# A decode product moved from VectorE to ScalarE and GpSimd, and half sums of k's exponentials for z in pairs three to nine

## The chip, the cores and the metric

The kernel runs on one core of a Trainium2 chip. The metric is the device time of one execution in microseconds (us); it is the median of several runs.

## The reference

Attention with a positive feature map feeds a two-layer network. In short, with 8 batches of 8 heads, 576 tokens, head size 64 and 128 features:

```python
def phi(x):
    proj = np.einsum('bhsd,df->bhsf', x, w_phi)
    proj = proj - np.max(np.abs(proj), axis=-1, keepdims=True)
    return np.concatenate([np.exp(proj), np.exp(-proj)], axis=-1)
q_p, k_p = phi(q), phi(k)
kv = np.einsum('bhsf,bhsd->bhfd', k_p, v)
z = np.sum(k_p, axis=2)
num = np.einsum('bhsf,bhfd->bhsd', q_p, kv)
den = np.einsum('bhsf,bhf->bhs', q_p, z)[..., None] + 1e-06
attn = num / den
...
x = attn.transpose(0, 2, 1, 3).reshape(4608, 512)
h = x @ w_in
g = np.maximum(h, 0.0) + alpha * np.minimum(h, 0.0)
out = g @ w_out
```

The weights `w_in` (512x2048) and `w_out` (2048x512) arrive as 64-bit numbers, two 32-bit words each, and are decoded on the chip.

## The kernel before

**Attention.** The work is cut into 32 pairs of heads, `attention_units(i)` for i = 0 to 31 (pair three of the title is i = 2). For a pair, `project(0)` and `project(1)` multiply ten tiles of tokens of k and q by `w_phi` on TensorE into PSUM (`pl` for the two short tiles, `pj` for eight). `pj` has one buffer. VectorE takes the largest magnitude (`m`, line 311) and subtracts it (`t`, line 312). ScalarE makes the exponentials of k (`xk`, four tiles, line 325, and `k`, the short one, line 320). `k_z` sums k's exponentials over the tokens by multiplying them with a matrix of ones on TensorE (line 365): for pairs i < 9 it takes all five tiles, four matmuls each. From pair 9 on, VectorE adds the five tiles up beforehand in `k_sum` (`y`, `z`, `z` again, lines 334, 338 and 341), and `k_z` has one tile left. `k_acc` makes kv (line 348), `kv_turn` and `q_turn` transpose (`kt`, `qt`), `q_exp` makes q's exponentials (`qf`, lines 402 and 404), `den` and `num` multiply them by z and kv (`d` line 431, `n` line 413). The denominators go through DRAM to be inverted (`r`, line 450) and spread (`rr`), and GpSimd multiplies them in (`s<-s,rr`, line 463).

**The two-layer network.** It runs in two passes over the tokens in chunks of 512. The first pass uses five of 16 slices of the hidden layer (`ffn1_units`) and is interleaved with the attention from pair 9 on. The second uses the other eleven and starts after the attention. Each operand is held as a high part and a low part (`gh` and `gl`, `xh` and `xl`), and three products are made of them.

**The decoding.** A block is 128x256 weights; there are 64, the first 20 within the attention-only start, two to a pair. `decode_load` brings in `raw`, whose last axis holds the low word and the high word. `decode_scale` (line 173) copies the high word with a factor on ScalarE. `decode_split` does four things on VectorE: a shift (181), an and-or that puts the sign in (182), a mask that leaves the exponent (183, `e`; the trace calls it `ew`), and a product of the low word with it (184). `decode_add` (189) adds that to the number on GpSimd. `decode_high` rounds it on ScalarE (123) and `decode_low` subtracts the rounded part on GpSimd (127). Blocks that do not stay in SBUF are written to `w_d`.

**The order.** Every step is put in a list with a due time by hand (`places(i)` for the attention; `WT` and `WL` for a block's steps after its time), and the list is sorted by it. The orders of TensorE, VectorE, ScalarE and SyncE are kept as they come; GpSimd's order is set by a scheduler.

Of the kernel before, what the change touches and what calls it, by code (L numbers as in the profile page):

```python
# [11 lines left out]
AF = mybir.ActivationFunctionType  # L12
ALU = mybir.AluOpType
# [39 lines left out]
XR_BUFS = 1  # L53
QH_BUFS = 2
ZP = 9


def places(i):
    early = i < ZP
    end = i >= NPAIR - 2  # L60
    return dict(
        ld=-1.90,
        lv=-0.80,
        p=(-0.9955 if early else -0.993, 0.0),
        ke=(-0.26, 0.0011),
        ks=(0.0015, 0.0022, 0.0026),
        kz=1.0002,
        ka=1.0012,
        ko=1.0025,
        kr=1.10,  # L70
        kc=1.16,
        q=(1.34, 1.50, 1.20),
        qe=(1.46, 1.62, 1.28),
        d=2.0004,
        ds=2.0008,
        n=2.005,
        s=2.0055,
        d9=2.25,
        dv=3.0016 if early else 3.20 if end else 2.80,
        rd=3.0017 if early else 3.21 if end else 2.82,  # L80
        rr=3.20 if early else 3.45 if end else 3.001,
        x=3.45 if early else 3.60 if end else 3.20,
        xs=3.90 if early else 3.85 if end else 3.45,
    )
# [24 lines left out]
def fused_kernel(ctx: ExitStack, tc: tile.TileContext, kq, v, w_phi, w_in, w_out, alpha, out):  # L109
    nc = tc.nc  # L110
    act, dve, pool, pe = nc.scalar, nc.vector, nc.gpsimd, nc.tensor
# [6 lines left out]
    def f(t):  # L118
        return t.bitcast(F32)
# [47 lines left out]
    wst = {}  # L167

    def decode_scale(ff, z, o, n):
        tag = f"w{ff}_{z}_{o}"  # L170
        raw = wraw.pop((ff, z, o))
        a = w1t.tile([P, n], U32, tag="wa", name=f"a{tag}", bufs=W_BUFS + 1)
        act.activation(f(a), raw[:, :, 1].bitcast(F32), AF.Copy, scale=2.0**-112)
        wst[ff, z, o] = [raw, a]

    def decode_split(ff, z, o, n):
        tag = f"w{ff}_{z}_{o}"
        raw, a = wst[ff, z, o][:2]
        lo, hi = raw[:, :, 0], raw[:, :, 1]
        e = w1t.tile([P, n], U32, tag="we", name=f"e{tag}", bufs=W_BUFS)  # L180
        dve.tensor_scalar(a, a, 3, None, op0=ALU.logical_shift_left)
        dve.scalar_tensor_tensor(a, hi, 0x80000000, a, op0=ALU.bitwise_and, op1=ALU.bitwise_or)
        dve.tensor_scalar(e, a, 0xFF800000, None, op0=ALU.bitwise_and)
        dve.scalar_tensor_tensor(f(e), lo, 2.0**-52, f(e), op0=ALU.mult, op1=ALU.mult)  # L184
        wst[ff, z, o] += [e]

    def decode_add(ff, z, o, n):
        _, a, e = wst[ff, z, o]
        pool.tensor_tensor(f(a), f(e), f(a), op=ALU.add)  # L189

    def decode_high(ff, z, o, n):
# [14 lines left out]
    def decode_store(ff, z, o, n):  # L206
# [4 lines left out]
    stages = dict(  # L211
        load=decode_load,
        scale=decode_scale,
        split=decode_split,
        add=decode_add,
        high=decode_high,
        low=decode_low,
# [54 lines left out]
    def attention_units(i):  # L272
        b, hp = divmod(i, NP)
        c = {}
# [51 lines left out]
            c["x", ch] = x  # L326

        def k_sum(step):
            if i < ZP:
                return  # L330
            x = c["x", 0].rearrange("p a h n f -> p (a h) (n f)")
            if step == 0:
                y = c["y"] = wk.tile([P, 4, 2 * FD], F32, tag="y", name=f"y{i}", bufs=1)
                dve.tensor_tensor(c["y"], x[:, :, : 2 * FD], x[:, :, 2 * FD :], op=ALU.add)
            elif step == 1:
                y = c["y"]
                c["zs"] = wk.tile([P, 4, FD], F32, tag="z", name=f"z{i}", bufs=1)
                dve.tensor_tensor(c["zs"], y[:, :, :FD], y[:, :, FD:], op=ALU.add)
            else:
                z = c["zs"]  # L340
                dve.tensor_tensor(z, z, c["x", 1].rearrange("p a h n f -> p (a h) (n f)"), op=ALU.add)
                c["z"] = z.rearrange("p (a h) f -> p a h f", a=2)
# [12 lines left out]

        def k_z():
            c["kv"] = ps_kv.tile([P, 3, FD], F32, tag="kv", name=f"kv{i}")
            if i < ZP:
                zs = [c["x", 0][:, :, :, j, :] for j in range(4)] + [c["x", 1][:, :, :, 0, :]]
            else:  # L360
                zs = [c["z"]]
            for j, z in enumerate(zs):
                for g in range(4):
                    h, a = divmod(g, 2)
                    pe.matmul(  # L365
                        c["kv"][32 * g : 32 * g + 32, 2],
                        lhsT=ones,
                        rhs=z[:, a, h, :],
                        start=j == 0,
                        stop=j == len(zs) - 1,  # L370
                    )
# [14 lines left out]
        def q_turn(h):  # L386
            pp, tag = (psf, "f") if i < ZP - 1 and h < 2 else (ps_m, "m")
            ps = c["qt", h] = pp.tile([P, 2 if h == 2 else 4, P], F32, tag=tag, name=f"qt{i}_{h}")
            if h == 2:
                for g in range(2):  # L390
                    pe.transpose(ps[:, g, :], c["t", 1][:, g, 0, :], ident)
            else:
                for j in range(4):
                    pe.transpose(ps[:, j, :], c["t", 1][:, h, 1 + j, :], ident)  # L394
# [70 lines left out]
        def store():  # L465
# [5 lines left out]
            (at["lv"], load_v),  # L471
            (at["ka"], k_acc),
            (at["kz"], k_z),
            (at["ko"], kv_out),
            (at["kr"], kv_turn),
# [14 lines left out]
        for n in range(3):  # L490
            us.append((at["ks"][n], lambda n=n: k_sum(n)))
            us.append((at["q"][n], lambda n=n: q_turn(n)))
            us.append((at["qe"][n], lambda n=n: q_exp(n)))
# [308 lines left out]
```

## Time and profile before

| | us |
|---|---|
| median of 3 runs | 1137.34 |
| lowest, highest | 1134.79, 1138.68 |
| the profiled execution | 1136.66 |
| its span in the trace | 1134.9 |

The page gives the busy time of each engine, its share in 40 slices, the transfers, the chain of work that ended last, and the costliest groups of instructions. The windows give the same busy times for chosen stretches, the timeline single instructions with the idle time before them and what ended it. Times count from the span's start. TensorE's clock stands at its full level (2.4 GHz, a granted clock of 1.00) after the first 50 us. The attention-only start lasts to about 105 us, the first pass to about 607 us, and the second pass to the end.

### The profile page before, as it was taken

What the parts mean: (1) busy time and instruction counts of PE and PEld (TensorE: products, weight loads), DVE (VectorE), ACT (ScalarE), POOL (GpSimd) and SP (SyncE); (2) the same over time, 40 slices, a digit from 0 to 9 for tenths busy, and PEclk for the clock granted to TensorE, in tenths of its full rate; (3) what the DMA queues carried; (4) which work ended last, traced back from release to release, by engine and by line L of the source; (5) the groups of instructions that cost most, each with busy time, mean ns of one, the idle gap of its engine ahead of it and who ended that gap; (6) DMA issues with size and microseconds to landing.
All of it is one profiled execution on the core that took longest, in us unless ns stands there. A gap on an engine that the chain in (4) does not pass through costs nothing.

```text
span 1134.9 us, 18362 instructions
## 1 busy us (share of the span) xinstructions
PE 1114.9 (98%) x7232; PEld 866.8 (76%) x7232; DVE 639.5 (56%) x978; ACT 561.2 (49%) x1149; POOL 214.5 (19%) x219
## 2 busy tenths in 40 slices
PE   7999999999999999999999999999999999999998
PEld 5766777777777777677778888888888888888886
DVE  7888867798788877835762432424242433333323
ACT  4777656666666765664553332424333333333332
POOL 1345332322424142243552000000000000000000
PEclk8999999999999999999999999999999999999999
DMA  5466264556446365466626130303030302020021
GB/s 188 142 184 216 80 194 147 171 163 205 145 163 199 94 214 168 146 197 213 231 74 211 69 112 1 111 1 111 1 112 1 111 1 80 33 79 33 3 72 38
DMA packets 74101, 133.68 MB, mean 118 GB/s; under 512 B 14624, under 2 KB 24480, under 8 KB 73376
## 3 DMA queue, kind: packets, MB, share of 16 engines
q1 hardware_dynamic: 71712, 122.48, 33.4%
q0 software_dynamic: 2016, 9.96, 2.6%
q8 instruction: 57, 0.93, 0.3%
q14 instruction: 28, 0.23, 0.1%
q10 hardware_dynamic: 288, 0.07, 0.0%
HBM read 93.92 MB, written 38.42 MB: 117 GB/s over the span
## 4 chain that ended last, share of the span: by engine, by line
PE 92%; DVE 4%; DMA 2%; ACT 1%; issue 0%; SPq 0%; ACTq 0%; DVEq 0%
PE h L503 11%; PE h L505 11%; PE h L504 11%; PE po L511 8%; PE po L509 8%; PE po L510 8%; PE kv L348 6%; PE pj L307 5%; PE n L413 5%; PE o L511 3%; PE o L509 3%; PE o L510 3%; PE d L431 3%; PE qt L394 2%; PE kv L365 2%; PE pl L307 1%
## 5 line engine op out<-in xcount | busy, mean ns | idle before, releaser
L240 DVE SCALAR_TENSOR_TENSOR g<-r,aln,g 128x512 f32<-128x512 f32 x144 | 111.0, 771 | 320.1 <-ACT g L236 319.8
L235 ACT ACTIVATE r<-h 128x512 f32<-128x512 f32 x144 | 86.5, 601 | 286.0 <-PE h L505 285.8
L127 DVE TENSOR_TENSOR gl<-g,gh 128x512 fp32r<-128x512 f32 x144 | 105.5, 732 | 73.0 <-ACT gh L123 72.5
L123 ACT CAST gh<-g 128x512 fp32r<-128x512 f32 x144 | 90.1, 625 | 88.1 <-DVE g L240 88.1
L236 ACT ACTIVATE g<-h 128x512 f32<-128x512 f32 x144 | 85.8, 596 | 2.8 <-DMA part_d<-os 2.8
L509 PE MATMUL po<-gh,wd 128*128 128x512 f32 x216 | 84.3, 390 | 0.0
L511 PE MATMUL po<-gl,wd 128*128 128x512 f32 x216 | 84.3, 390 | 0.0
L510 PE MATMUL po<-gh,wd 128*128 128x512 f32 x216 | 84.3, 390 | 0.0
L311 DVE TENSOR_REDUCE m<-pj 128x8 f32<-128x1024 f32 (+1 forms) x66 | 78.2, 1185 | 7.0 <-PE pj L307 6.7
L307 PE MATMUL pj<-w_sb,raw 64*128 64x128 f32 x1024 | 74.2, 286 | 7.8 <-DMA w_sb<-w_phi_dram 4.1
L307 PEld LDWEIGHTS pj<-w_sb,raw 64*128 64x128 f32 x1024 | 65.0, 194 | 21.4 <-issue 14.1
L189 POOL TENSOR_TENSOR aw<-ew,aw 128x256 f32<-128x256 f32 x64 | 56.7, 887 | 128.6 <-DVE ew L184 128.6
L312 DVE TENSOR_TENSOR t<-pj,m 128x1024 f32<-128x1024 f32 (+1 forms) x66 | 78.7, 1192 | 2.3
L509 PE MATMUL o<-gh,w 128*128 128x512 f32 x180 | 75.9, 422 | 1.9 <-ACT os L554 1.7
L503 PE MATMUL h<-xh,w 128*128 128x512 f32 x180 | 75.8, 421 | 0.0
L463 POOL TENSOR_TENSOR s<-s,rr 128x576 f32<-128x576 f32 x32 | 48.5, 1517 | 140.6 <-DMA rr<-rec_d 120.2
L511 PE MATMUL o<-gl,w 128*128 128x512 f32 x180 | 71.6, 398 | 3.2 <-DVE gl L127 3.0
L511 PE MATMUL po<-gl,w 128*128 128x512 f32 x180 | 70.3, 391 | 1.5 <-DVE gl L127 1.4
L404 ACT ACTIVATE qf<-qt 128x512 f32<-128x512 f32 x128 | 68.5, 616 | 6.3 <-PE qt L394 6.3
L505 PE MATMUL h<-xl,w 128*128 128x512 f32 x180 | 70.7, 393 | 0.0
L510 PE MATMUL o<-gh,w 128*128 128x512 f32 x180 | 70.6, 392 | 0.0
L504 PE MATMUL h<-xh,w 128*128 128x512 f32 x180 | 70.5, 392 | 0.0
(105 smaller groups left out, 2408.8 us busy)
## 6 DMA issues: line engine op xcount, KB each, us to landing
xr<-x_d SPq DMA_DIRECT2D x18, 1024.0 KB
raw<-kq_dram SPq DMA_DIRECT2D x31, 576.0 KB
v<-v_dram SPq DMA_DIRECT2D x32, 320.0 KB
w_d<-raww SPq DMA_DIRECT2D x38, 256.0 KB
rr<-rec_d SPq DMA_DIRECT2D x64, 144.0 KB
x_d<-s SPq DMA_DIRECT2D x32, 288.0 KB
part_d<-os SPq DMA_DIRECT2D x36, 256.0 KB
pt<-part_d SPq DMA_DIRECT2D x9, 1024.0 KB
```

The costliest lines, as they stand in the source:

```text
L123: return act.copy(dst, src)
L127: return eng.tensor_tensor(dst, src, f(hi), op=ALU.subtract)
L235: act.activation(st["r"], ps, AF.Relu, scale=-1.0)
L236: act.activation(st["g"], ps, AF.Relu)
L240: dve.scalar_tensor_tensor(g, st["r"], aln[:, ff : ff + 1], g, op0=ALU.mult, op1=ALU.add)
L307: pe.matmul(dst[h, j], lhsT=c["raw"][hs, ts], rhs=w_sb[hs], start=True, stop=True)
L503: pe.matmul(ps, lhsT=wt[0][:, ws], rhs=xh, start=n == 0, stop=False)
L504: pe.matmul(ps, lhsT=wt[1][:, ws], rhs=xh, start=False, stop=False)
L505: pe.matmul(ps, lhsT=wt[0][:, ws], rhs=xl, start=False, stop=n == NK - 1)
L509: pe.matmul(ps, lhsT=wt[2][:, ws], rhs=gh, start=first, stop=False)
L510: pe.matmul(ps, lhsT=wt[3][:, ws], rhs=gh, start=False, stop=False)
L511: pe.matmul(ps, lhsT=wt[2][:, ws], rhs=gl, start=False, stop=last)
```

## The change

In the decoding, ScalarE gets a second activation for a block: it converts the low word to a float and multiplies it by the constant factor, in place in `raw`. The product with `e` goes from VectorE to GpSimd, ahead of the addition there. For z, VectorE now makes `y` (two tiles of `xk` added to two others) for pairs 2 to 8 as well, and `k_z` takes `y` as two tiles and the short tile, three in all, where it took five.

```diff
+ZY = 2
...
         act.activation(f(a), raw[:, :, 1].bitcast(F32), AF.Copy, scale=2.0**-112)
+        act.activation(f(raw)[:, :, 0], raw[:, :, 0], AF.Copy, scale=2.0**-52)
         wst[ff, z, o] = [raw, a]
...
-        lo, hi = raw[:, :, 0], raw[:, :, 1]
+        hi = raw[:, :, 1]
...
         dve.tensor_scalar(e, a, 0xFF800000, None, op0=ALU.bitwise_and)
-        dve.scalar_tensor_tensor(f(e), lo, 2.0**-52, f(e), op0=ALU.mult, op1=ALU.mult)
         wst[ff, z, o] += [e]
 
     def decode_add(ff, z, o, n):
-        _, a, e = wst[ff, z, o]
+        raw, a, e = wst[ff, z, o]
+        pool.tensor_tensor(f(e), f(raw)[:, :, 0], f(e), op=ALU.mult)
         pool.tensor_tensor(f(a), f(e), f(a), op=ALU.add)
...
         def k_sum(step):
-            if i < ZP:
+            if i < ZY or i < ZP and step > 0:
                 return
...
-            if i < ZP:
+            if ZY <= i < ZP:
+                y = c["y"].rearrange("p (a h) (n f) -> p a h n f", a=2, n=2)
+                zs = [y[:, :, :, j, :] for j in range(2)] + [c["x", 1][:, :, :, 0, :]]
+            elif i < ZP:
                 zs = [c["x", 0][:, :, :, j, :] for j in range(4)] + [c["x", 1][:, :, :, 0, :]]
```

On VectorE, between the projections of pairs 5 and 6, before:

```order
L312 TENSOR_TENSOR t5_1_814<-pj5_1_817,m5_1_2_834 128x2x512
L450 RECIPROCAL r9_2_881<-d9_2_773 128x9
L181 TENSOR_SCALAR aw4_0_0_808<-aw4_0_0_808 128x256
L182 SCALAR_TENSOR_TENSOR aw4_0_0_808<-raww4_0_0_780,aw4_0_0_808 128x256
L183 TENSOR_SCALAR ew4_0_0_886<-aw4_0_0_808 128x256
L184 SCALAR_TENSOR_TENSOR ew4_0_0_886<-raww4_0_0_780,ew4_0_0_886 128x256
L311 TENSOR_REDUCE m6_0_0_901<-pj6_0_892 128x8
```

and with the change (all lines from the decoding on are one to five higher):

```order
L314 TENSOR_TENSOR t5_1_813<-pj5_1_816,m5_1_2_833 128x2x512
L336 TENSOR_TENSOR y5_872<-xk5_803 128x1024
L455 RECIPROCAL r9_2_874<-d9_2_770 128x9
L183 TENSOR_SCALAR aw4_0_0_806<-aw4_0_0_806 128x256
L184 SCALAR_TENSOR_TENSOR aw4_0_0_806<-raww4_0_0_778,aw4_0_0_806 128x256
L185 TENSOR_SCALAR ew4_0_0_879<-aw4_0_0_806 128x256
L313 TENSOR_REDUCE m6_0_0_893<-pj6_0_884 128x8
```

`y` stands ahead of the reciprocal of an earlier pair, and the product behind the mask is gone.

On ScalarE, between the transpose of pair 3's kv and its q exponentials, before:

```order
L384 COPY sf3_763<-kt3_756 128x384
L173 ACTIVATE aw3_0_256_775<-raww3_0_256_648 128x256
L402 ACTIVATE qf3_777<-qt3_2_768 128x2x64 x2
L123 CAST w3_93<-aw3_0_0_646 128x256
L404 ACTIVATE qf3_777<-qt3_0_782 128x512 x2
L404 ACTIVATE qf3_777<-qt3_1_791 128x512 x2
```

and with the change:

```order
L389 COPY sf3_760<-kt3_752 128x384
L174 ACTIVATE aw3_0_256_772<-raww3_0_256_651 128x256
L175 ACTIVATE raww3_0_256_651<-raww3_0_256_651 128x256
L407 ACTIVATE qf3_775<-qt3_2_765 128x2x64 x2
L124 CAST w3_93<-aw3_0_0_648 128x256
L409 ACTIVATE qf3_775<-qt3_0_780 128x512 x2
L409 ACTIVATE qf3_775<-qt3_1_789 128x512 x2
```

One activation more stands ahead of all six that make `qf`.

On GpSimd, the two blocks of one pair and the multiplication `s` of an earlier one, before:

```order
L189 TENSOR_TENSOR aw3_0_0_646<-ew3_0_0_724,aw3_0_0_646 128x256
L463 TENSOR_TENSOR s1_590<-s1_590,rr1_765 128x576
L127 TENSOR_TENSOR w3_93<-aw3_0_0_646,w3_93 128x256
L189 TENSOR_TENSOR aw3_0_256_775<-ew3_0_256_796,aw3_0_256_775 128x256
L127 TENSOR_TENSOR w3_93<-aw3_0_256_775,w3_93 128x256
```

and with the change:

```order
L190 TENSOR_TENSOR ew3_0_0_721<-raww3_0_0_620,ew3_0_0_721 128x256
L191 TENSOR_TENSOR aw3_0_0_648<-ew3_0_0_721,aw3_0_0_648 128x256
L468 TENSOR_TENSOR s1_590<-s1_590,rr1_762 128x576
L128 TENSOR_TENSOR w3_93<-aw3_0_0_648,w3_93 128x256
L190 TENSOR_TENSOR ew3_0_256_794<-raww3_0_256_651,ew3_0_256_794 128x256
L191 TENSOR_TENSOR aw3_0_256_772<-ew3_0_256_794,aw3_0_256_772 128x256
L128 TENSOR_TENSOR w3_93<-aw3_0_256_772,w3_93 128x256
```

Five instructions for a pair become seven; behind `s` a product stands between the subtraction of one block and the addition of the next.

## Rows read from the trace of the kernel before

**Rows 1.** The page, part 1: busy time, share of the span, instructions.
```profile
PE 1114.9 (98%) x7232; PEld 866.8 (76%) x7232; DVE 639.5 (56%) x978; ACT 561.2 (49%) x1149; POOL 214.5 (19%) x219
```

**Rows 2.** Windows: stretch, length, busy time of each engine, clock, DMA share, GB/s.
```profile
50.00:100.00 50.00, 48.62 (x617) 33.72 (x613) 42.01 (x74) 36.45 (x87) 21.54 (x24) 1.00 0.67 203
...
200.00:250.00 50.00, 50.00 (x419) 36.39 (x417) 40.49 (x59) 32.80 (x71) 17.10 (x15) 1.00 0.54 171
```

**Rows 3.** The chain in order of time: start, duration, what (z's matmuls).
```profile
35.27 1.23 PE kv L365 x40
...
66.99 1.23 PE kv L365 x40
...
77.57 1.23 PE kv L365 x40
...
101.29 1.23 PE kv L365 x40
```

**Rows 4.** Timeline, TensorE, one pair: start, duration, line, tiles, idle time before.
```profile
66.92 1.08 PE L365 MATMUL kv<-xk,ones 128*32 128x128 f32 x32
...
67.82 0.40 PE L365 MATMUL kv<-k,ones 128*32 128x128 f32 x8
...
69.12 1.95 PE L348 MATMUL kv<-xk,v 128*64 128x256 f32 x16
```

**Rows 5.** Timeline, ScalarE, the same pair.
```profile
65.00 0.44 ACT L173 ACTIVATE aw<-raww 128x256 f32<-128x256 f32 x1
...
65.34 0.43 ACT L402 ACTIVATE qf<-qt 128x128 f32<-128x128 f32 x2
...
65.95 2.07 ACT L404 ACTIVATE qf<-qt 128x512 f32<-128x512 f32 x4
```

**Rows 6.** Timeline at 89 us, where `d` waited for `qf`.
```profile
89.43 1.56 ACT L404 ACTIVATE qf<-qt 128x512 f32<-128x512 f32 x3
...
91.04 0.14 PEld L431 LDWEIGHTS d<-qf,sf 128*32 128x32 f32 x4 [0.33 <-ACT qf L404]
...
91.65 1.95 PE L348 MATMUL kv<-xk,v 128*64 128x256 f32 x16
```

**Rows 7.** Timeline, VectorE and GpSimd, the same pair as in rows 4.
```profile
65.54 0.29 DVE L181 TENSOR_SCALAR aw<-aw 128x256 uint32<-128x256 uint32 x1 [0.99 <-ACT aw L173]
...
66.73 0.43 DVE L184 SCALAR_TENSOR_TENSOR ew<-raww,ew 128x256 f32<-128x256 uint32 x1
...
70.51 0.21 DVE L450 RECIPROCAL r<-d 128x9 f32<-128x9 f32 x1
70.62 0.83 POOL L127 TENSOR_TENSOR w<-aw,w 128x256 fp32r<-128x256 f32 x1 [0.79 <-ACT w L123]
...
70.90 0.83 DVE L182 SCALAR_TENSOR_TENSOR aw<-raww,aw 128x256 uint32<-128x256 uint32 x1
```

**Rows 8.** `y` at 105 us; then lines 334 and 189: ns min/median/max, first and last start.
```profile
104.95 1.68 DVE L334 TENSOR_TENSOR y<-xk 128x1024 f32<-128x1024 f32 x1
105.52 2.25 POOL L127 TENSOR_TENSOR xl<-xr,xh 128x512 fp32r<-128x512 f32 x1
...
L334 DVE TENSOR_TENSOR y<-xk x23: 1215/1216/2212, 105.0 to 480.1; 128x1024 f32<-128x1024 f32 x23
...
L189 POOL TENSOR_TENSOR aw<-ew,aw x64: 717/738/1648, 20.1 to 597.3; 128x256 f32<-128x256 f32 x64
```

**Rows 9.** Timeline: a reciprocal on VectorE, and the `s` that uses it.
```profile
59.94 0.21 DVE L450 RECIPROCAL r<-d 128x9 f32<-128x9 f32 x1
...
66.76 1.68 POOL L463 TENSOR_TENSOR s<-s,rr 128x576 f32<-128x576 f32 x1 [3.94 <-DMA rr<-rec_d]
```

**Rows 10.** Timeline, later: two waits of TensorE and the product ahead of one.
```profile
152.10 0.50 PE L509 MATMUL o<-gh,w 128*128 128x512 f32 x1 [1.72 <-ACT os L554]
...
540.27 0.42 DVE L184 SCALAR_TENSOR_TENSOR ew<-raww,ew 128x256 f32<-128x256 uint32 x1
...
541.36 0.50 PE L511 MATMUL po<-gl,w 128*128 128x512 f32 x1 [1.38 <-DVE gl L127]
```

## The prediction

> **What bounds the kernel now.** I read the page's busy times first: TensorE is busy for 1114.9 of 1134.9 us, VectorE, ScalarE and GpSimd for 56%, 49% and 19% [rows 1]. Idle time of the other three therefore costs nothing, unless TensorE waits for it. Second, the windows: between 50 and 100 us TensorE is busy for 48.62 of 50 us and VectorE for 42.01, in the steady stretch at 200 us for 50.00 and 40.49 [rows 2]. So the attention-only part at the start is the place where VectorE, too, is nearly full. Third, the chain of waits in that part: it consists of TensorE alone, and a pair takes 77.57 - 66.99 = 10.58 us [rows 3], from one group of `z` matmuls to the next. I call this the period of a pair. Whatever lengthens or shortens it between about 35 and 105 us lengthens or shortens the whole, because TensorE is full behind it.
>
> All durations below come from the profiled execution (1136.66 us, its span 1134.9). The median of the three runs is 1137.34, 0.68 us above it; the forecast is made for the median. About 0.3% (3.4 us) is what a measurement of this kernel can tell from no change.
>
> **Part 1: z by half sums on TensorE.** For pairs 2 to 8 the 16 matmuls of `xk` with `ones` become 8. Each shows as two records. The 32 records start at 66.92 and the next group at 67.82 [rows 4]: 0.90 us. Half of that is 0.45 us a pair, 3.15 us for seven pairs. TensorE is on the path, so this is the whole possible gain of this part. It is 0.28% of the time.
>
> **Part 2: the product's first half on ScalarE.** 64 more activations of 128x256, two a pair. The trace has no strided write of this kind; the nearest row is the activation of the same form, which starts at 65.00 with the next instruction following at 65.34 [rows 5]: 0.34 us of ScalarE's time each. Lower bound 0 (if it fits into a wait), upper 0.45 (its duration). I take 0.34, the row of the same shape and stride. Where it stands matters more. One of the two stands between the scaling and the six activations that make `qf`, the last of which ends at 65.95 + 2.07 = 68.02 [rows 5]. The `d` matmuls read `qf`. How tight that is can be read at 89 us, where `d` really waited: the last `qf` ended at 89.43 + 1.56 = 90.99, and the first matmul after `d` started at 91.65 [rows 6], 0.66 us later. In the undisturbed pair the same matmul starts at 69.12 [rows 4], 1.10 us behind its `qf`; so the slack is 0.44 us. Part 1 takes 0.45 us of it away (TensorE arrives earlier) and part 2 another 0.34. TensorE then waits 0.45 + 0.34 - 0.44 = 0.35 us a pair, and of the 0.45 us saved 0.10 remain: period 10.48. This is the step on which I rest most: the saving is given back at `d`.
>
> **Part 3: VectorE.** In a period of 10.58 VectorE waits 0.99 us, before the shift of the second block [rows 7], and is busy for 9.59. The change takes away two products of 0.43 each [rows 7] and adds one `y`, 1.22 us where nothing disturbs it [rows 8]. That gives 9.59 - 0.86 + 1.22 = 9.95 us. It would fit into 10.48 with 0.53 to spare. `y` itself is used a whole period later, so TensorE doesn't wait for it; what it delays is the projection's reduce and subtract behind it, and TensorE's next projection waits for those, since `pj` has one buffer.
>
> **Part 4: GpSimd, and what it does to VectorE.** 64 more products of 128x256 on GpSimd. The row for the same shape with contiguous operands is 0.74 us [rows 8]; with one operand of stride two the trace shows none. Bounds 0.72 (the shortest of that row) and 1.65 (the longest); I take 0.74. By itself this costs nothing: in the stretch from 50 to 100 us GpSimd is busy for 21.54 of 50 [rows 2], and ten products would add 7.4. But a VectorE instruction and a GpSimd one that both work in SBUF do not overlap. The shift-and-or at 70.90 took 0.83 us instead of 0.43, beside a GpSimd subtraction that had begun at 70.62 [rows 7]; and the `y` at 104.95 took 1.68, while the GpSimd subtraction that began at 105.52 took 2.25 us [rows 8]. The Trainium skill says in "SBUF — State Buffer", section "SBUF: two separate sides", that the two engines share a pair of ports by an exclusive lock, held for the whole instruction, and that the loser is fully blocked; these two pairs of rows agree.
>
> So I ask whether `y` meets GpSimd. `s<-s,rr` starts when its `rr` lands, 6.82 us after the reciprocal (59.94, then 66.76), and lasts 1.68 [rows 9]. The reciprocal now stands behind `y`, so `s` moves about 1.2 us later in the pair. Behind it stand a subtraction, the new product and the addition: 66.8 + 1.2 + 1.7 (`s`) + 0.7 (the subtraction) puts the product at about 70.4 and the addition at 71.1 in the terms of the pair shown, and `y` begins where the reciprocal stands now, at 70.51 [rows 7]. A collision with the product or the addition is to be expected in each pair. One more collision costs VectorE up to 0.74: 9.95 + 0.74 = 10.69 us. Two would give 11.43. None gives 9.95, and then the period is the 10.48 of part 2. I take one, since the additions that follow the second block's split lie under reads of PSUM, which the rows don't show to collide. Period 10.69 instead of 10.58: 0.11 us lost a pair.
>
> **Part 5: the later blocks.** 44 of the 64 blocks are decoded after the start, under a TensorE that is full. There only TensorE's few waits count: for `gl` of VectorE at 541.36 (1.38 us), with a product of 0.42 us just before that `gl`, and for ScalarE at 152.10 (1.72 us), which waits for a transfer and doesn't change [rows 10]. Without the product `gl` comes about 0.4 us earlier. Lower bound: four such waits for `gl` shrink by 0.43 each, -1.7 us. Upper bound: they grow by a GpSimd instruction each, +3.0. I take -0.4, for the one place where the removed product stands next to the wait.
>
> **The sum.** Pairs 2 to 6 (their `z` matmuls stand from 35.27 to 77.57 us [rows 3]): 5 x 0.11 = +0.55. Pair 7: its `d` is the one that waited for the late `qf` [rows 6], so an earlier TensorE only waits longer: 0. Pair 8: its `z` lies at 101.29 us [rows 3], next to the full stretch; I let it keep its 0.45. The later blocks: -0.4. Together -0.3 us, 1136.4 in terms of the profiled execution, **1137.0 us** in terms of the median: no change that can be told.
>
> **Rivals.**
> *The saving goes through.* If the new activation hides in a wait of ScalarE, and GpSimd's instructions fall under VectorE's reads of PSUM, nothing stands against part 1. For it: VectorE's own sum, 9.95, is below 10.13 (10.58 - 0.45), so with no collision it can follow. Against it: the slack of 0.44 at `d`. Time: 3.15 us less, and two later waits shorter by 0.43: 1137.34 - 4.0 = 1133.3. Chance 0.18.
>
> *VectorE becomes the bound through collisions.* `y` waits for a GpSimd instruction, another enters between `y` and the shift behind it, and so the sum reaches 9.95 + 2 x 0.74 = 11.43 us a pair, 0.85 more than now. It decides from the point where collisions cost more than 0.63 us a pair (9.95 + 0.63 = 10.58). For it: three GpSimd instructions (product, addition, subtraction) stand in a row at that place. Against it: a longer period lets GpSimd finish before the next `y`. Five pairs of it make +4.25, and one later wait longer by 0.74: 1137.34 + 5.0 = 1142.3. Chance 0.20. The lock named above, if it holds for every one of these instructions, is the rule under which this rival wins.
>
> That the change doesn't do what it says is excluded by the order of the instructions: TensorE's groups of 16 are groups of 8 in seven pairs, and VectorE has one instruction less in each block.
>
> **How the numbers follow.** My forecast has a chance of 0.62, the two rivals 0.18 and 0.20. The range reaches from a little below the first (1133.3, with one later wait less) to the second: 1132.8 to 1142.5. The forecast's own range, between periods of 10.48 and 11.0, is 1135.5 to 1140.0, all of it within 0.3%. So faster by more than 0.3% has 0.18, within 0.3% 0.62, slower 0.20.
>
> **What would show it.** Part 1 is right if the `kv<-y,ones` groups take about 0.45 us. Part 2 is right if `d` waits for `qf` in the steady pairs, by about 0.35 us where VectorE is not the later one; wrong if the chain still shows no wait there. Part 4 is right if `y` lasts well over 1.22 us in pairs 3 to 8 and TensorE's `pj` waits for `t`; wrong if `y` has its bare duration. If the period between 35 and 78 us comes out at 10.13, the first rival holds; at 11 or more, the second. The prediction as a whole is wrong if the stretch up to 105 us changes by more than 3 us, or if the waits behind 450 us do.

## The result, and the profile after

The changed kernel took 1139.56 us (median of 10 runs, 1138.45 to 1141.98) against 1137.31 for the kernel before beside it (10 runs): a ratio of 1.0023 with an interval of 1.0014 to 1.0033. It is slower by 2.25 us. That is small, but outside the interval, where the forecast was no change, a little on the fast side. The profiled execution has a span of 1137.7 us, 2.8 more than before.

The page, part 1, of the changed kernel [answers to rows 1]:

```profile
PE 1114.8 (98%) x7120; PEld 865.7 (76%) x7120; DVE 621.2 (55%) x921; ACT 582.3 (51%) x1213; POOL 272.8 (24%) x283
```

Work moved as the change says: VectorE has 18 us less, ScalarE 21 more, GpSimd 58 more. TensorE has 112 instructions less and the same busy time. (The busy time is modelled, and a matmul that waits inside a group counts as busy.) So the question is where it stood still.

The windows of the changed kernel [answers to rows 2]:

```profile
50.00:100.00 50.00, 46.86 (x541) 31.79 (x537) 45.20 (x70) 40.22 (x100) 31.76 (x34) 1.00 0.67 202
200.00:250.00 50.00, 49.91 (x412) 36.63 (x410) 38.31 (x56) 33.69 (x75) 19.66 (x19) 1.00 0.55 175
```

In the attention-only part TensorE is busy for 1.8 us less than before in the same window, 46.86 against 48.62. The steady stretch has hardly moved.

To find the places, I compared the start of the first group of `kv<-xk,v` in each pair, after minus before (from the two timelines; a step in this offset is time lost or gained between two pairs):

| pair | 1 | 2 | 5 | 6 | 7 | 8 | 9 | 11 | 14 | 29 | 30 | end |
|---|---|---|---|---|---|---|---|---|---|---|---|---|
| offset, us | -0.87 | -0.98 | -1.29 | -0.39 | -0.06 | -0.06 | +1.79 | +2.09 | +2.42 | +2.41 | +1.78 | +2.8 |

The changed kernel is 1.29 us ahead at pair 5, 0.87 of it from ahead of pair 1, and loses 3.1 between pairs 5 and 9. Behind that the account is nearly even: +0.6 up to pair 14, -0.6 at pair 30, +1.0 up to the end.

**The gain.** The chain of the changed kernel, steady pairs [answers to rows 3]; start, duration, what:

```profile
34.39 0.79 PE kv L370 x24
35.19 1.30 PE d L436 x16
36.49 2.31 PE kv L350 x20
...
44.87 0.79 PE kv L370 x24
45.66 1.30 PE d L436 x16
```

The same step of the chain before:

```profile
36.50 0.97 PE d L431 x16
```

`z` takes 0.79 us instead of 1.23, so 0.44 is saved. `d` takes 1.30 instead of 0.97, so 0.33 is given back: it waits for `qf` between its matmuls (the run with the new activation behind `qf`, below, shows this). The period is 44.87 - 34.39 = 10.48 instead of 10.58.

**The loss.** The timeline of the changed kernel between pairs 8 and 9; start, duration, engine, line, and in brackets the idle time before and what ended it:

```profile
102.50 1.43 POOL L468 TENSOR_TENSOR s<-s,rr 128x576 f32<-128x576 f32 x1 [2.82 <-DMA rr<-rec_d]
103.88 1.28 POOL L128 TENSOR_TENSOR xl<-xr,xh 128x512 fp32r<-128x512 f32 x1
104.86 1.38 DVE L336 TENSOR_TENSOR y<-xk 128x1024 f32<-128x1024 f32 x1
105.13 1.71 POOL L128 TENSOR_TENSOR w<-aw,w 128x256 fp32r<-128x256 f32 x1
106.80 1.18 POOL L190 TENSOR_TENSOR ew<-raww,ew 128x256 f32<-128x256 f32 x1
108.06 0.72 POOL L191 TENSOR_TENSOR aw<-ew,aw 128x256 f32<-128x256 f32 x1
108.82 0.40 ACT L124 CAST w<-aw 128x256 fp32r<-128x256 f32 x1 [3.18 <-POOL aw L191]
109.13 0.40 ACT L446 ACTIVATE ds<-d 128x288 f32<-128x288 f32 x1
109.43 0.71 ACT L322 ACTIVATE k<-t 64x256 f32<-64x256 f32 x2
110.04 0.46 ACT L380 COPY ks<-kv 128x384 f32<-128x384 f32 x1
110.56 0.55 PE L385 MATMUL kt<-ident,ks 128*128 128x128 f32 x3 [1.79 <-ACT ks L380]
```

The same block before:

```profile
104.83 0.72 POOL L189 TENSOR_TENSOR aw<-ew,aw 128x256 f32<-128x256 f32 x1
105.58 0.40 ACT L123 CAST w<-aw 128x256 fp32r<-128x256 f32 x1 [0.45 <-POOL aw L189]
106.81 0.46 ACT L375 COPY ks<-kv 128x384 f32<-128x384 f32 x1
```

Read it from the bottom. TensorE's `kt` waits 1.79 us for `ks`. `ks` depends on nothing new, but ScalarE's order is fixed, and three places ahead of it stands the rounding `cast w`, which waited 3.18 us for GpSimd's addition. The addition comes 3.2 us later than before (108.06 against 104.83). About 1.0 of it is `s`, which started at 102.50 instead of 101.51, since its `rr` landed later (the reciprocal now stands behind `y`; that was not tried apart). Another 1.0 is the subtraction `w` of the other block, which used to take 0.72, began 0.27 us after `y` and took 1.71. Behind it came the new product, which took 1.18; the addition began 1.26 after it. GpSimd's order is otherwise that of the kernel before: the second `xl` stands behind the addition in both. At 74.33 us the same chain costs 0.94.

In the last stretch the rounding stands ahead of other work of ScalarE:

```profile
525.47 0.40 ACT L124 CAST raww<-aw 128x256 fp32r<-128x256 f32 x1 [4.47 <-POOL aw L191]
525.78 1.07 ACT L559 COPY os<-o 128x512 f32<-128x512 f32 x2
526.41 0.50 PE L514 MATMUL o<-gh,w 128*128 128x512 f32 x1 [0.79 <-ACT os L559]
...
556.68 0.41 ACT L124 CAST raww<-aw 128x256 fp32r<-128x256 f32 x1 [7.11 <-POOL aw L191]
...
558.12 0.50 PE L508 MATMUL h<-xh,w 128*128 128x512 f32 x1 [1.07 <-ACT g L238]
```

And the two waits of [rows 10], in the changed kernel, with what ScalarE waited for ahead of the first, at 153 us:

```profile
153.07 0.62 ACT L124 CAST xh<-xr 128x512 fp32r<-128x512 f32 x1 [3.00 <-DMA xr<-x_d]
154.23 0.50 PE L514 MATMUL o<-gh,w 128*128 128x512 f32 x1 [2.05 <-ACT os L559]
...
543.07 0.50 PE L516 MATMUL po<-gl,w 128*128 128x512 f32 x1 [0.92 <-DVE gl L128]
```

**The theory (A).** What stands ahead of TensorE's producer (the instruction whose result it waits for) in ScalarE's order decides. GpSimd's addition is late, the rounding waits for it, and `ks` (later `os` and `g`) waits behind the rounding, without needing it. The same holds for ScalarE's cast of x, which waits for a transfer with `qf` and `os` behind it. **The rival:** the load and the collisions of VectorE and GpSimd decide, so the order on ScalarE has no price. The expectations call the rival theory B, or name one that fits the run.

### The profile page after: what moved, and what is told of

Its sections match the earlier page's. It is cut to its first block, busy times and chain, and to the rows that moved or that the text cites. A ratio compares the mean times of both kernels' runs of the same rounds, so it can differ in the third digit from the quotient of the medians.

```text
span 1137.7 us, 18267 instructions
## 1 busy us (share of the span) xinstructions
PE 1114.8 (98%) x7120; PEld 865.7 (76%) x7120; DVE 621.2 (55%) x921; ACT 582.3 (51%) x1213; POOL 272.8 (24%) x283
## 3 DMA queue, kind: packets, MB, share of 16 engines
q0 software_dynamic: 2016, 9.96, 2.5%
## 4 chain that ended last, share of the span: by engine, by line
PE 83%; DMA 6%; DVE 5%; ACT 3%; issue 2%; POOL 1%; SPq 0%; DVEq 0%; ACTq 0%; POOLq 0%
PE h L508 11%; PE h L510 11%; PE h L509 10%; PE po L516 8%; PE po L514 8%; PE po L515 8%; PE kv L350 5%; PE pj L309 5%; PE n L418 4%; PE o L516 3%; PE o L514 3%; PE o L515 3%; PE d L436 2%; PE qt L399 2%; DMA rr<-rec_d 2%
## 5 line engine op out<-in xcount | busy, mean ns | idle before, releaser
L190 POOL TENSOR_TENSOR ew<-raww,ew 128x256 f32<-128x256 f32 x64 | 56.8, 887 | 103.8 <-DVE ew L185 40.5
```

## The experiments

### One part of the change at a time

The part on z alone: the decoding is that of the kernel before. Against the changed kernel, the main lines:

```diff
-        act.activation(f(raw)[:, :, 0], raw[:, :, 0], AF.Copy, scale=2.0**-52)
...
+        dve.scalar_tensor_tensor(f(e), lo, 2.0**-52, f(e), op0=ALU.mult, op1=ALU.mult)
...
-        pool.tensor_tensor(f(e), f(raw)[:, :, 0], f(e), op=ALU.mult)
```

> Only the z part (y for pairs 2 to 8 on VectorE, two tiles fewer on TensorE); the decoding is as before. Theory A (the loss comes from ScalarE's queue: a rounding that waits for GpSimd's late addition stands ahead of ks, and TensorE's kt waits for ks): no added wait of kt near 110 us; VectorE is busy 9.59 + 1.22 = 10.81 us a pair and so sets a period of about 10.8 in pairs 2 to 6, the rest as before; 1137.3 to 1138.8 us. Theory B (the additional y on VectorE makes the loss): the whole loss is here, 1139.5 us or more, and TensorE's waits after 105 us grow as in the changed kernel.

Measured: 1141.39 us, ratio 1.0038 (1.0024 to 1.0052), slower than before. The time is the one that theory B named (1139.5 or more); theory A had named 1137.3 to 1138.8. Two waits of TensorE from its timeline:

```profile
56.43 1.16 PE L308 MATMUL pj<-w_sb,raw 64*128 64x128 f32 x16 [0.47 <-DVE t L313]
...
92.77 0.68 PE L435 MATMUL d<-qf,sf 128*32 128x288 f32 x4 [1.66 <-ACT qf L408]
```

A part of the loss is VectorE's, as B has it. With both products and `y`, VectorE is too long: `pj` waits for `t`, 0.19, 0.47, 0.46 and 0.72 us, and the offset to the kernel before goes from +0.35 at pair 2 to +1.18 at pair 6, where z should have gained. The larger step, +2.57 from pair 6 to pair 7, is at the second row: `qf` stands there behind a cast of x that waited 3.20 us for its transfer, and behind the gap the granted clock reads 0.92 and 0.74 in the windows from 90 to 100 us. (Why that transfer was late was not tried apart.) No wait of `kt` for `ks` over 0.1 us is left, as A expected. So `y` alone doesn't make the waits at `kt`, but it has a price of its own while both products stay on VectorE.

The decoding alone: `y` only from pair 9 on, as before.

```diff
-ZY = 2
+ZY = 9
```

> Only the decoding part (low words scaled on ScalarE, product on GpSimd); z as before. Theory A: the wait of kt for ks near 109 us is there (1 us or more), the second half of the first pass gains about 1 us of waits for ScalarE, the period up to 80 us stays at 10.57 (ScalarE's 0.34 fits into the slack of 0.44); 1139 to 1140 us. Theory B: no loss, 1137.3 us or less, since VectorE only loses work.

Measured: 1143.15 us (4 runs), ratio 1.005 (1.0032 to 1.0067). Both theories had named less (A 1139 to 1140). The period stayed at 10.57, and the time went where TensorE waited for ScalarE: 1.24 us for `ks` at 99.6 (not near 109, where it was expected; there it lost nothing), 0.95 for `qf` at 90.9, 1.97 for `os` at 530, and at 154 us

```profile
154.58 0.56 PE L514 MATMUL o<-gh,w 128*128 128x512 f32 x1 [2.51 <-ACT os L559]
```

with this window right behind:

```profile
155.00:160.00 5.00, 5.00 (x28) 3.85 (x27) 0.43 (x3) 3.92 (x7) 3.88 (x4) 0.67 0.71 220
```

After that idle time the granted clock was 0.67 of full speed for 5 us, 1.65 us of work; behind the wait at 530 it read 0.66, another 1.7. The two falls make about half of the 6.8 us by which this trace is longer than the one before. Each part alone is slower than the kernel before: z needs the time that the decoding frees on VectorE, and the decoding by itself adds waits and saves TensorE nothing.

### The order on ScalarE

The rounding behind `ks`: for the second block of each pair up to 10 it comes later in the program.

```diff
+WE = dict(WT, high=0.504)
...
-        return [(t + (WT if t < TL else WL)[k], ...
+        return [(t + (WE if t < 11 and t % 1 > 0.25 else WT if t < TL else WL)[k], ...
```

> The changed kernel, with the rounding of each odd block of the first 20 put behind ks in ScalarE's queue. Theory A: the waits of kt for ks (0.94, 0.54 and 1.79 us at 73, 97 and 109 us) fall below 0.3 each, and the time falls by about 2 us to 1137.5 us. Theory B: the waits stay or come back as waits for VectorE, 1139.5 us.

Measured: 1139.96 us, ratio 1.0023 (1.0011 to 1.0035): no gain in the time, where A had named 1137.5 and the rival 1139.5. In the trace, all waits of `kt` for `ks` are gone, and pair 9 starts at -1.31 instead of +1.79 us. The rounding still waits for the addition, but `ks` stands ahead of it now:

```profile
105.27 0.47 ACT L381 COPY ks<-kv 128x384 f32<-128x384 f32 x1
107.03 0.41 ACT L125 CAST w<-aw 128x256 fp32r<-128x256 f32 x1 [1.28 <-POOL aw L192]
...
151.49 0.62 ACT L125 CAST xh<-xr 128x512 fp32r<-128x512 f32 x1 [3.74 <-DMA xr<-x_d]
...
152.64 0.58 PE L515 MATMUL o<-gh,w 128*128 128x512 f32 x1 [2.80 <-ACT os L560]
```

The last two rows say where most of it went. (Of the 3.4 us from pair 9 to pair 11, 0.8 go ahead of pair 10.) At 151 us ScalarE's cast of x waits for its transfer, which doesn't come earlier because TensorE does (151.49 against 150.94 before), and `os` stands behind that cast. TensorE's gap grew from 1.72 to 2.80, and behind it the clock was low:

```profile
150.00:155.00 5.00, 2.36 (x6) 1.90 (x7) 0.21 (x1) 3.52 (x7) 2.16 (x2) 0.79 0.74 180
155.00:160.00 5.00, 5.00 (x53) 3.43 (x54) 2.20 (x5) 1.98 (x4) 3.02 (x3) 0.87 0.64 198
```

From pair 11 on the offset is +2.09, as in the changed kernel. Theory A is right on the cause at 109 us, but a second wait of the same kind, and the fall of the clock behind it, took all of it back.

ScalarE's new activation of the second block behind `qf`:

```diff
+WE = dict(WT, lows=0.13)
...
     def decode_scale(ff, z, o, n):
         ...
-        act.activation(f(raw)[:, :, 0], raw[:, :, 0], AF.Copy, scale=2.0**-52)
+    def decode_lows(ff, z, o, n):
+        raw = wst[ff, z, o][0]
+        act.activation(f(raw)[:, :, 0], raw[:, :, 0], AF.Copy, scale=2.0**-52)
```

> The changed kernel, with ScalarE's new activation of each odd block of the first 20 put behind the six exponentials that make qf. If that activation ahead of qf is what keeps the period at 10.47 us: the period of pairs 2 to 5 falls to 10.13 to 10.25, and d has no wait there; the time stays at 1139 to 1140 us all the same, since the lead is lost at 89 us (transfer) and at kt. If instead VectorE or GpSimd sets 10.47, the period does not change.

Measured: 1140.85 us, ratio 1.0025 (1.0013 to 1.0037). `d` no longer waits in the steady pairs, and from pair 1 to pair 3 the period is 10.15 us (the offset goes from -0.51 to -0.94 to -1.36): the activation ahead of `qf` is what kept it at 10.48. But GpSimd's product now starts later, and the rounding with it. `kt` waits for `ks` four times, 0.77, 0.66, 1.41 and 1.75 us, for instance:

```profile
85.59 0.55 PE L390 MATMUL kt<-ident,ks 128*128 128x128 f32 x3 [1.41 <-ACT ks L385]
```

The wait moved from one producer on ScalarE to the next.

### The casts of x out of the way

Four kernels have ScalarE's first cast of x behind `qf` in chunk 0 and behind the two `os` in chunk 1: the kernel before, the changed kernel, the one with the rounding behind `ks`, and that one with the new activation behind `qf` as well.

```diff
-FX0 = (1.80, 1.35, 0.95, 0.45)
+FX0 = (1.58, 1.35, 0.95, 0.45)
+FX1 = (0.82, 0.75, 0.55, 0.35)
...
-        ... [t0 - dt for dt in (FX if b else FX0)])
+        ... [t0 - dt for dt in (FX if b > 1 else FX1 if b else FX0)])
```

> The kernel before, with one thing moved: ScalarE's cast of the first piece of x stands behind qf in chunk 0 and behind the two os in chunk 1, so that neither waits for the transfer of x. Theory A (what TensorE lost or could not keep is decided by what stands ahead of its producer in ScalarE's queue): the gaps at about 90 us (0.21 + 0.30, d for qf) and at 150 us (1.71, for os) go, the time falls by 1.5 to 2.3 us, to 1135.0 to 1135.8. Rival (the transfers of x themselves gate TensorE, the queue does not matter): the same idle time turns up a little later, at the first matmul that reads x, and the time stays at 1137.3.

> The changed kernel with the same move of the two casts of x. Theory A: the gaps for qf at 88.5 and 90.2 (0.97 + 0.30) and for os at 152 (2.05) go, the waits of kt for ks stay (0.94 at 73, 1.79 at 109) since the rounding still stands ahead of ks. Time 1136.0 to 1137.5, below the changed kernel by 2 to 3.3 us. Rival (the loss comes from the collisions of VectorE and GpSimd): nothing that collides is moved, so the time stays at 1139 to 1140.

> The changed kernel with the rounding of the weights' words behind ks (as in the run with the late rounding) and the same move of the two casts of x. Theory A: no wait of kt for ks, none of d for qf at 89, none for os at 150 and so no fall of the clock behind it; the start of pair 11 stands 2 to 3.5 us ahead of the kernel before and keeps this to the end, but for the waits of the last third: 1134.0 to 1136.0. Rival (time gained before 110 us is given back whatever the order, because the transfers are the bound there): the gap at 150 us stays at 2.8 and the time at 1139 to 1140.

> The run before this one, and ScalarE's new activation of each pair's second block (pairs up to 10) behind qf. Theory A: neither d nor kt waits in the steady pairs, so the period falls from 10.47 towards 10.13, pair 6 starts 2 to 2.5 us ahead of the kernel before, and the time is 1133.0 to 1135.0. Rival (VectorE with 9.95 us and its collisions is next): pj waits for t by 0.2 to 0.5 in each pair, the period stays at 10.4 to 10.5 and the time equals that of the run before this one.

| kernel | us | ratio to before | interval |
|---|---|---|---|
| before, casts moved | 1134.70 | 0.997 | 0.9957 to 0.9982 |
| changed, casts moved | 1137.26 | 0.9992 | 0.9982 to 1.0001 |
| and rounding behind `ks` | 1136.11 | 0.9979 | 0.9966 to 0.9993 |
| and activation behind `qf` | 1135.64 | 0.9977 | 0.9967 to 0.9988 |

The gaps at 90 and 150 us are gone in all four, and no clock fell at 150 us. The first gained more than was expected (3.5 us; a part of it, some 1.2, lies ahead of pair 0), the second came out as expected, the third just above the upper edge, and the fourth took the time that its rival named, that of the third. In the fourth the period fell to about 10.15 in pairs 1 to 3 (the offset goes from -0.14 to -0.56 to -0.99), and then VectorE was the next, up to pair 6:

```profile
86.66 1.16 PE L315 MATMUL pj<-w_sb,raw 64*128 64x128 f32 x16 [0.36 <-DVE t L320]
```

Its largest loss, 2.4 us from pair 7 to pair 8, is again ScalarE's: 0.95 for `ks`, 1.38 for `s` (now behind a rounding) and 0.39 for `qf`.

Moving the cast of chunk 0 has its own price: in the first kernel pair 7 gains 1.4 us and pair 8 loses 1.8, since `xk`, and with it `ks` and `t`, come later. So for chunk 0 the rival was right (the idle time turns up a little later, here as 1.25 us for `ks` at 95.8 and 1.59 for `t` at 99.5), and theory A for chunk 1, where the 1.72 us are gained and kept. The 1.2 us ahead of pair 0 lie where the move touches nothing.

### The last blocks, and the control

First, the rounding later in both places and the cast of x moved in chunk 1 alone; second, the control, the kernel before with that last move; third, the first again, but with the last 17 blocks decoded as before the change; fourth, the third with the rounding back ahead of `ks`.

```diff
+FX1 = (0.82, 0.75, 0.55, 0.35)
+WE = dict(WT, high=0.504)
-WL = dict(..., high=0.60, low=0.80, store=0.95)
+WL = dict(..., high=0.92, low=0.99, store=1.07)
...
```

> The changed kernel with the rounding of the words behind ks in the pairs up to 10, with the rounding of the last blocks later in the program (behind os and g), and with ScalarE's cast of the first piece of x behind os in chunk 1 alone; chunk 0 stays as it is in the changed kernel. Theory A (ScalarE's order decides): the offset to the kernel before is about -1.3 us at pair 9 as in the run with the late rounding, -3 at pair 11 since the wait for os at 150 us (1.7 us in the kernel before) goes, and no wait for os or g of ScalarE over 0.4 us stands behind 500 us: 1133.5 to 1135.5. Rival (the load of VectorE and GpSimd decides, and a wait that is taken away turns up elsewhere): 1137 or more.

> The kernel before with the cast of x behind os in chunk 1 alone. It is the control for the run before: what that one gains over this one is the change's own part. Theory A: the gap of 1.71 us at 150 us goes and nothing else moves: 1135.5 to 1136.5. Rival (the wait there is for the transfer, not for the order): 1137.3 to 1138.

The third, against the first (the two places where `on_dve` leaves the new activation and GpSimd's product out are not shown):

```diff
-WL = dict(..., high=0.92, low=0.99, store=1.07)
+WL = dict(..., high=0.60, low=0.80, store=0.95)
...
+        if t >= TL:
+            on_dve.add(blk)
...
+        if (ff, z, o) in on_dve:
+            dve.scalar_tensor_tensor(f(e), raw[:, :, 0], 2.0**-52, f(e), op0=ALU.mult, op1=ALU.mult)
```

> The first run of this call with the decode of the last 17 blocks as in the kernel before (both products in one VectorE instruction, rounding at its old place). Theory A: behind 480 us the waits are those of the kernel before (1.54, 0.77 and 1.38 us for gl, none over 0.4 for os or g), 0.5 to 1.2 us more than in the first run: 1134.5 to 1136.5. Rival (the new product on GpSimd does what harm is done in the late stretch, wherever the rounding stands): 0.5 to 1.5 us less than in the first run.

> The run with the last 17 blocks on VectorE, with one thing put back: the rounding of the words stands ahead of ks again in the pairs up to 10, as in the changed kernel. Theory A: kt waits for ks again, by 0.9 us at about 73 and 1.8 us at about 109, and pair 9 starts about 3 us later than with the rounding behind ks; that is kept to the end, so 1137 to 1138, 2.5 to 3.5 us more than that run's 1134.55. Rival (once the waits for x and the waits of the last blocks are gone, the place of the rounding has no price): 1134 to 1135.5.

| kernel | us | ratio to before | interval |
|---|---|---|---|
| later roundings, x of chunk 1 | 1139.33 | 1.002 | 1.0004 to 1.0035 |
| control: before, x of chunk 1 | 1135.77 | 0.998 | 0.9966 to 0.9994 |
| last 17 blocks on VectorE | 1134.55 | 0.998 | 0.9966 to 0.9995 |
| the same, rounding ahead of `ks` | 1136.23 | 0.9994 | 0.9983 to 1.0004 |

The first missed: 1137 or more was its rival's time. Pair 9 stands at +0.45 where about -1.3 was expected (`qt` waits 0.88 us for `s`, which is now behind the rounding), pair 11 at -1.27 where -3 was, and pair 30 at -1.58, but the end at +4.2: behind 500 us it loses 5.8, of which 3.5 are gaps beyond those of the kernel before, and 1.7 a fall of the clock. Its timeline there:

```profile
529.32 0.43 ACT L176 ACTIVATE aw<-raww 128x256 f32<-128x256 f32 x1 [2.36 <-DMA raww<-w_out_dram]
...
532.63 0.59 ACT L561 COPY os<-o 128x512 f32<-128x512 f32 x1 [2.54 <-DMA part_d<-os]
533.27 0.50 PE L510 MATMUL h<-x2hl,w 128*128 128x512 f32 x1 [1.08 <-ACT os L561]
...
545.30 0.50 PE L516 MATMUL po<-gh,w 128*128 128x512 f32 x1 [1.28 <-ACT gh L126]
...
569.77 0.67 PE L518 MATMUL o<-gl,w 128*128 128x512 f32 x1 [1.30 <-DVE gl L130]
```

and the window behind the last of these:

```profile
570.00:575.00 5.00, 5.00 (x16) 3.94 (x16) 3.51 (x4) 1.77 (x5) 4.25 (x4) 0.66 0.31 105
```

Here the rounded words go back into `raw`. With a later rounding the buffer comes free later, the next block's load lands later, and ScalarE stands at that load with `os` behind it; `os` itself then waits for the transfer of an earlier `os`, and in SyncE's order, which is fixed too, that transfer stands behind the loads and stores of the blocks (the rows fit this; it was not tried apart). So in the last stretch a later place for the rounding made new waits. With the product back on VectorE and the rounding back at its old place for these blocks, no wait for `os`, `g` or `gh` over 0.1 us is left behind 500 us in the third kernel; what is left are waits for `gl` of 0.77, 2.00 and 0.54, with a fall of the clock (0.66 from 540 to 545 us) behind the second. The changed kernel has the rounding at that same old place and waits for `os` and `g`. So here the product on GpSimd, and the late addition with it, does the harm, as the third run's rival has it; that run was 4.8 us below the first, where theory A had named 0.5 to 1.2 more.

The fourth tells what the rounding's place is worth once the later gaps no longer swallow it. Its timeline and window:

```profile
111.06 0.55 PE L394 MATMUL kt<-ident,ks 128*128 128x128 f32 x3 [2.04 <-ACT ks L389]
```

```profile
110.00:115.00 5.00, 3.94 (x16) 3.31 (x17) 4.15 (x6) 3.47 (x12) 3.23 (x5) 0.69 0.96 298
```

The wait is back, and here the clock fell behind it; pair 9 stands at +3.88 instead of +0.08. The medians differ by 1.7 us where 2.5 to 3.5 were expected, and the two intervals overlap, so the times don't tell the two kernels apart, and the price of the rounding's place is shown by the rows alone. One reason for the smaller size stands in the trace with the late rounding: at 109.17 `qt` waits 1.31 us for ScalarE's `s`, which is now the one behind the rounding.

**What is best.** The kernel before with both casts of x moved (1134.70, 0.997) and the changed kernel with chunk 1's cast moved, the rounding behind `ks` and the last blocks on VectorE (1134.55, 0.998) beat both kernels. The first is not shown to beat the control, which moves chunk 1's cast alone: what its trace has more up to pair 6, 1.5 us, lies ahead of pair 1. Against the control (0.998) the second shows no gain that can be told: the half sums and the moved product bring about 1.2 us in the medians at best, and most of what was found lies in the cast of x, which the change didn't touch.

## Why the prediction was wrong

**Part 1** was right: `z` takes 0.79 instead of 1.23 us, 0.44 where 0.45 stood.

**Part 2** was right: `d` gives back 0.33 (0.35 forecast), and the period is the 10.48 that it named for VectorE without a collision. It was called the step on which the forecast rests most; it holds from pair 1 to pair 5, and the run with the activation behind `qf` (10.15) shows the cause.

**Part 3 and 4** had the collisions right and their price wrong. `y` took 1.73 and 1.68 us in two of the steady pairs, and 1.22 to 1.23 in two others. But `pj` didn't wait for `t` there, since the forecast of VectorE's sum was too high. These windows are two steady pairs, the fourth number being VectorE's busy time:

```profile
44.87:55.35 10.48, 10.48 (x125) 7.18 (x125) 9.96 (x16) 8.79 (x22) 6.60 (x7) 1.00 0.62 190
55.35:65.84 10.49, 10.49 (x129) 7.29 (x125) 10.07 (x17) 8.79 (x22) 6.61 (x7) 1.00 0.65 195
```

It is 9.96 and 10.07 with the collisions in, where 10.69 was forecast. The term of 9.59 for the pair before is the mis-sized one: it took the period less one wait, and a window of one pair in the trace before shows 9.06 busy:

```profile
45.84:56.42 10.58, 10.58 (x146) 7.49 (x149) 9.06 (x18) 8.07 (x21) 4.54 (x6) 1.00 0.64 194
```

From there the same steps give 9.06 - 0.86 + 1.22 = 9.42, and one collision of 0.5 (`y` at 1.73 instead of 1.22) makes it 9.92, near what was measured. So the period of 10.69, and the +0.55 for pairs 2 to 6, failed.

The step that failed for the whole is in Part 4 as well: "By itself this costs nothing" of GpSimd's new product. The collision was priced for VectorE, the engine that had been looked at. The other side of it, GpSimd's `w` and product stretched to 1.71 and 1.18 us, was left out, and so was what the later `s` does to the addition (108.06 instead of 104.83). Part 2 had asked for `qf` what stands ahead of it on ScalarE; the same was not asked for `ks`, which stands behind the rounding, which waits for the addition: +0.9 at pair 6 and +1.85 at pair 9, and neither is in the sum. The Trainium skill states in "SBUF — State Buffer", section "SBUF: two separate sides", that of a VectorE instruction with two inputs in SBUF and a GpSimd one, whichever starts first has the shared ports for its whole instruction and the other is blocked; the row of `w` at 105.13 (1.71 us), behind `y` at 104.86, agrees, with GpSimd as the loser.

**Pair 7** was forecast at 0 and lost 0.33; **pair 8** was to keep 0.45 and kept nothing that shows (-0.06 in both). There `y` took 2.33 us, and VectorE was busy from it up to `t` without a break, so TensorE waited for `t`:

```profile
100.51 1.16 PE L309 MATMUL pj<-w_sb,raw 64*128 64x128 f32 x16 [0.91 <-DVE t L314]
```

Before, this wait was 0.18. The wait at 152 us, which "doesn't change", grew from 1.72 to 2.05.

**Part 5** was right in its mechanism and half of the account. `gl`'s waits shrank from 1.54 to 0.92 and from 1.38 to 0.92, as the removed product said. But ScalarE's `os` and `g` stand now behind a late rounding (0.79 and 1.07 us of TensorE's time; a third wait, 0.35 for `os` at 602.73, has none ahead of it). So what lies behind pair 29 costs +0.4 net (-0.6, then +1.0) instead of -0.4; the bounds of -1.7 and +3.0 held it.

**What was not forecast at all** is the gain ahead of pair 1, -0.87: in the start `pj` waits for `t` 0.96 us where it was 2.09, and the clock, at 0.63 and 0.68 from 10 to 20 us in the trace before, did not fall there. How much of it is the change's isn't shown: 0.28 is the first matmul, which started at 3.84 instead of 4.12 us, and two traces of the kernel before with a cast of x moved, whose start is the same, stand at -1.14 (both casts) and +0.32 (the control) there.

Of the rivals, "the saving goes through" fails at `d` as its own "against" said. "VectorE becomes the bound" fails as a whole; in the changed kernel it came true in pair 8 alone, and in part in the run with z alone. The time lies inside the range, and inside the forecast's own part of it, but by another mechanism than any of the three cases: that is luck. The sum had the wrong sign (-0.3 us against +2.25), and the measurement could tell a smaller difference than the 3.4 us that the prediction names.

## What to carry to other kernels

When an instruction is moved to an engine with time to spare, follow its result to the first engine that waits for it in a fixed order, and list what stands behind that wait; a late result costs what its neighbours in the queue cost, not what its reader costs. Price a collision between two engines for both of them. And before trusting a gain ahead of a wait for a transfer, take that wait away first: time gained in front of it only lengthens it, and a longer gap can cost the clock on top.

## What was not expected of the hardware

The granted clock fell to its half level (1.2 GHz) behind some gaps of TensorE and not behind others of nearly the same length. In the traces with a window shown above it read 0.67 behind 2.51 us, 0.79 and 0.87 behind 2.80, 0.66 behind 1.30, 0.69 behind 2.04; in the changed kernel it stayed at 1.00 behind 2.05 us at 152 and behind 1.79 at 109. A window of half a microsecond in the last run, with its half level, and one of the changed kernel behind its gap of 2.05:

```profile
112.00:112.50 0.50, 0.50 (x3) 0.41 (x2) 0.41 (x1) 0.50 (x3) 0.00 (x0) 0.50 0.86 192
...
155.00:160.00 5.00, 5.00 (x56) 3.52 (x56) 2.37 (x6) 3.57 (x6) 4.04 (x4) 1.00 0.67 219
```

By the windows above that hold a whole fall (0.67; 0.79 with 0.87; 0.66) it cost 1.65 to 1.7 us (0.33 of 5 us in the first), more than the gap ahead of it where that was 1.30. The length of the gap alone doesn't decide between the two cases; what does stays open.
